# A retention block and a tanh-shrink MLP on one core: weights first, and another order of the opening

## The chip, the cores and the metric

The kernel runs on one core of one Trainium2 chip. A core has TensorE (matrix products, PE in the profile; its weight loads are PEld), VectorE (DVE), ScalarE (ACT), GpSimd (POOL) and SyncE (SP), which here only issues DMA transfers. Each engine works through its own instructions in order; semaphores tie them together. The metric is device time in microseconds, the median over runs.

## The reference

Inputs are q, k, v of shape (4, 8, 768, 64) in float32, w_in of (512, 2048) and w_out of (2048, 512), both in float64, and the output is (3072, 512) in float32.

```python
gamma = 1.0 - 2.0 ** (-5.0 - np.arange(H))          # H = 8 heads
for t in range(S):                                   # S = 768, D = 64
    state = gamma * state + k[:, :, t] (outer) v[:, :, t]
    y[:, :, t] = (1 / sqrt(D)) * q[:, :, t] @ state
x = y.transpose(0, 2, 1, 3).reshape(B * S, H * D)    # 3072 x 512
h = x @ w_in                                         # 3072 x 2048
out = (h - tanh(h)) @ w_out                          # 3072 x 512
```

## The kernel before

**Chunks.** The 3072 tokens are 24 chunks of 128; six chunks make one batch entry. A chunk's k, q and v are 128 tokens x 512 (8 heads of 64). The decay is folded into q and v: they are multiplied by tables of powers of gamma (`scale`, L236). k and q are turned so that a head's 64 features lie on partitions, either by TensorE (`turn`, L250, four 128x128 transposes each for k and q, then copied to SBUF by ScalarE in `turn_copy`, L262 and L264) or by a DMA that transposes 16-bit words (`turn_by_dma`: ScalarE splits the words into the buffer `apart`, L273; SP writes them to DRAM, L276, and reads them back transposed, L278). `apart` has one buffer. Then `products` makes k'v for the state and k q' for the scores (L298, L304, 32 passes each), VectorE masks the scores (L311) and adds up the state (L321 to L327), and `outputs` with `outputs_rest` forms y in PSUM (L352). `see` reads four single columns of it on ScalarE (L382), which orders the second part behind the first, and `keep_x` copies y to xT (L393), four chunks to a tile.

**Weights.** There are 32 weight tiles of 512 KB as float64. Tiles come in eights: four of w_in (128 columns each), then four of w_out (128 rows each). A tile is loaded by SP, in three DMAs for w_in and one for w_out (L154, L149). It is turned into float32 by hand: ScalarE takes the two words apart (`convert_begin`, L172, L173), VectorE puts the bits together in four instructions (`convert_bits`, L181 to L187), and GpSimd or VectorE does the last multiply and add (`convert_end`, L195, L199). The first three tiles, and those from 9 on, use three staging buffers; tiles 3 to 8 use spare room that later holds xT.

**Steps.** The MLP goes in 96 steps, each 256 tokens (n) by 256 hidden columns (m2). `up` is two half steps of eight passes (L414) into one PSUM bank of tag `h`, of which there are two. ScalarE makes the square, the tanh and three factors (`shrink_begin`, `shrink_factors`, L423 to L433); VectorE does six instructions (`shrink_multiply`, `shrink_end`, L439 to L453), the fifth of which is the last to read the bank. `down` is eight passes of 128x512 (L462), two steps later in the plain loop. The first steps go (0,0), (0,1), (1,0), (1,1), (2,0), (2,1), (3,0), (3,1); step 8 is (3,2).

**The order.** Steps 0 to 7 and chunks 0 to 7 are written out by hand as a string of pieces, a letter and a number each, which are emitted in that order to all engines' queues. L loads a chunk, W a weight tile, s and w scale q and v, t and T turn k and q, c and C copy what was turned, K turns by DMA, p, m and z are products, mask and state, b, e, r and y are the outputs, `see`, the rest and the copy to xT. A, D and G are the three parts of a conversion. u and v are a step's two half steps, a, q, d and g its four parts on ScalarE and VectorE, o its down and E the copy of its sums. x counts zero products that the next group of PE work runs ahead of itself: `keep_busy` multiplies a tile of zeros, in a PSUM bank that is about to be overwritten. From step 8 on (`BEGUN`) a plain loop sets the order, and chunks from 8 on are turned by DMA.

PSUM banks of tag `t` (the later turned k and q, and the products) are one pair, so each group waits until the last has been read. k and q have two SBUF buffers each, v four, so SP's load of chunk 2 waits until chunk 0 has been used, and what is behind it on SP waits too. SP also waits, before each DMA, for the eighth DMA before it.

Of the kernel before, what the change touches and what calls it, by code (L numbers as in the profile page):

```python
# [16 lines left out]
P = 128  # L17
# [7 lines left out]
B0, C0 = 1.1162213056058772, 5.494931718829769  # L25
B1, C1 = -1.609711559785289, 5.546157850574988
# [6 lines left out]
def kernel(  # L33
# [20 lines left out]
    nc = tc.nc  # L54
# [28 lines left out]
    def bank(tag, name):  # L83
        return ps.tile([P, BANK], F32, tag=tag, name=name)
# [8 lines left out]
    at = [0]  # L93
# [6 lines left out]
    busy = cst.tile([P, P], F32, name="busy")  # L100
# [9 lines left out]
    w1 = wts.tile([P, NC, DF], F32, name="w1")  # L110
    w2 = wts.tile([P, NM, DM], F32, name="w2")
# [78 lines left out]
    def convert_end(i, engine):  # L190
        if i not in words:
            return
        dst, src = weight_ends(i)
        head, low, power = words.pop(i)
        engine.tensor_tensor(low, low, power.bitcast(F32), op=ALU.mult)  # L195
        head = head.bitcast(F32)
        if isinstance(src, list):
            low, head = (t.rearrange("p (c n) -> p c n", c=NC) for t in (low, head))
        engine.tensor_tensor(dst, low, head, op=ALU.add)  # L199
# [5 lines left out]

    idle = [0]

    def keep_busy(at):  # L210
        for _ in range(idle[0]):
            nc.tensor.matmul(at, busy, busy, start=True, stop=True, skip_group_check=True)  # L212
        idle[0] = 0


    loaded = {}
# [15 lines left out]
    def scale(ci, which, engine):  # L232
        if ci >= NCH:
            return
        t, g = loaded[ci][1 + which], (gq, gv)[which]
        engine.tensor_tensor(t, t, g[:, ts(ci % CPB, H)][:, :, None].to_broadcast([P, H, D]),  # L236
                             op=ALU.mult)

    def turn(ci, which, early=False):

        if early:
            tp = bank("o", f"kqTp{which}_{ci}")
        else:
            if which == 0:
                turned[ci] = banks("t", f"kqTp_{ci}")
            tp = turned[ci][:, which]
        keep_busy(tp[:, :P])
        t = loaded[ci][which]
        for p in range(NP):
            nc.tensor.transpose(tp[:, ts(p, P)],  # L250
                                t[:, ds(2 * p, 2)].rearrange("p h d -> p (h d)"), ident)
        if early:
            turned.setdefault(ci, []).append(tp)
# [31 lines left out]
    scores = {}  # L285

    def products(ci):

        kh, _, vh = loaded[ci]
        kT, qT = (sides[ci][:, i] for i in range(2))  # L290
        sp = banks("t", f"s_{ci}")
        keep_busy(sp[:, 0, :P])
        scores[ci] = halves = sp.rearrange("p r (w n t) -> p r w n t", w=2, n=NP)
        for p in range(NP):
            for a in range(2):
                for i in range(2):
                    h, r = 2 * p + i, ds(D * a, D)
                    nc.tensor.matmul(halves[ds(D * i, D), a, 1, p], kh[r, h], vh[r, h],  # L298
                                     start=True, stop=True, skip_group_check=True)
        for p in range(NP):  # L300
            for a in range(2):
                for i in range(2):
                    r = ds(D * i, D)
                    nc.tensor.matmul(halves[ds(D * a, D), i, 0, p], kT[r, p, ts(a, D)],  # L304
                                     qT[r, p, ts(a, D)], start=True, stop=True,
                                     skip_group_check=True)
# [7 lines left out]
        masked[ci] = m  # L314

    def state(ci):
        halves = scores.pop(ci)
        j = ci % CPB
        if j == 0:
            states[ci] = mid.tile([P, 2, NP, D], F32, tag="state", name=f"state_{ci}", bufs=3)  # L320
            nc.vector.tensor_copy(states[ci][:, 1], halves[:, 0, 1])  # L321
        else:
            nc.vector.tensor_tensor(states[ci][:, 1], halves[:, 0, 1], states[ci][:, 0],
                                    op=ALU.add)
        if j < CPB - 1:
            nxt = mid.tile([P, 2, NP, D], F32, tag="state", name=f"state_{ci + 1}", bufs=3)
            nc.vector.tensor_tensor(nxt[:, 0], halves[:, 1, 1], states[ci][:, 1], op=ALU.add)  # L327
            states[ci + 1] = nxt
# [7 lines left out]
    def outputs(ci):  # L336

        j = ci % CPB
        vh = loaded[ci][2]
        turned.pop(ci, None)  # L340
        qT = sides.pop(ci)[:, 1]
        a_, st = masked.pop(ci), states.pop(ci)
        y = y_banks[:, ci % 2]
        keep_busy(y[:, 0, 0])
        begun = set()

        def to_y(p, i, a, lhsT, rhs):

            col, r = (i + p) % 2, (ci + p) % 2
            start = (r, col) not in begun  # L350
            begun.add((r, col))
            nc.tensor.matmul(y[ds(D * col, D), r, p // 2, ts(a, D)], lhsT, rhs,  # L352
                             start=start, stop=True, skip_group_check=True)

        def intra(first):
            for pp in range(NP // 2):
                for i in range(2):
                    for a in range(2):

                        for col in range(2):  # L360
                            p = 2 * pp + ((a + col) % 2 if first else (a + col + 1) % 2)
                            if (i + p) % 2 != col:
                                continue
                            r = ds(D * a, D)
                            to_y(p, i, a, vh[r, 2 * p + i], a_[r, i, p])

        for a in range(2):
            if j or a:
                for p in range(NP):
                    for i in range(2):  # L370
                        r = ds(D * i, D)
                        to_y(p, i, a, st[r, a, p], qT[r, p, ts(a, D)])
        intra(True)
        halfway[ci] = intra
# [25 lines left out]
    o_p = {}  # L400
# [6 lines left out]
    def up(n, m2, i):  # L407

        if i == 0:
            hps[n, m2] = bank("h", f"h_{n}_{m2}")  # L410
        hp = hps[n, m2][:, ts(i, TH)]
        keep_busy(hp[:, :P])
        for c in range(NC):
            nc.tensor.matmul(hp, w1[:, c, ts(2 * m2 + i, P)], xT[n // 2][:, c, ts(n % 2, TH)],  # L414
                             start=(i == 0 and c == 0), stop=(c == NC - 1),
                             skip_group_check=True)
# [39 lines left out]
    def down(n, m2, j, first, last):  # L456

        if first:
            o_p[j] = bank("o", f"o_{n}_{m2}_{j}")
            keep_busy(o_p[j][:, :P])  # L460
        for i in range(2):
            nc.tensor.matmul(o_p[j], gT[n, m2][:, i, ts(j, P)], w2[:, 2 * m2 + i],  # L462
                             start=(first and i == 0), stop=(last and i == 1))
# [74 lines left out]

    BEGUN = 8
    EARLY_TURNS = 4  # L540
    TO_VECTOR = 2

    def tall(ci):
        return nc.vector if ci < TO_VECTOR else nc.gpsimd

    pieces = {
        "L": load_chunk,
        "W": load_weights,
        "s": lambda c: scale(c, 0, tall(c)),
        "w": lambda c: scale(c, 1, tall(c)),  # L550
        "t": lambda c: turn(c, 0, c < EARLY_TURNS),
        "T": lambda c: turn(c, 1, c < EARLY_TURNS),
        "c": lambda c: turn_copy(c, 0),
        "C": lambda c: turn_copy(c, 1 if c < EARLY_TURNS else None),
        "K": turn_by_dma,
        "p": products,
        "m": mask,
        "z": state,
# [3 lines left out]
        "y": keep_x,  # L562
        "A": convert_begin,
        "D": convert_bits,
        "G": lambda i: convert_end(i, tall(i)),
        "u": lambda s: up(*steps[s][:2], 0),
        "v": lambda s: up(*steps[s][:2], 1),
        "a": lambda s: shrink_begin(*steps[s][:2]),
# [3 lines left out]
        "o": lambda s: [down(*steps[s][:2], j, *steps[s][2:]) for j in range(2)],  # L572
        "E": lambda s: [add_up(*steps[s][:2], j) for j in range(2)],
        "x": lambda n: idle.__setitem__(0, n),
    }
    if w_out.dtype != F32:
        rooms += [xp.tile([P, 2, 2 * BANK], U32, tag="xT", name=f"raws_{i}") for i in range(3)]
    order = """
    L0 x8 t0 c0 s0 x5 T0 w0 L1 C0 x3 t1 W0 p0 c1 s1 m0 x2 T1 z0 W1 C1 w1 x3 b0 p1 e0 A0 r0
    m1 z1 y0 A1 D0 L2 x4 b1 t2 e1 c2 G0 r1 s2 y1 D1 x3 T2 w2 L3 u0 C2 W2 p2 G1 s3 t3 m2 T3  # L580
    w3 c3 v0 z2 C3 b2 A2 L4 p3 e2 W3 D2 a0 r2 s4 y2 w4 q0 W4 m3 z3 G2 x9 t4 b3 A3 d0 T4 e3
    C4 r3 g0 L5 y3 x1 p4 A4 W5 u2 D3 s5 v2 W6 w5 m4 D4 u1 G3 a2 q2 z4 L6 x6 t5 d2 G4 T5 A5
    v1 W7 C5 g2 b4 s6 a1 W8 p5 w6 e4 u3 D5 q1 L7 W9 W10 W11 K6 v3 m5 A6 G5 z5 r4 a3 d1 b5 y4 e5
    o0 s7 g1 w7 A7 D6 q3 K7 r5 D7 G6 y5 x3 u4 d3 v4 G7 A8 g3 p6 a4 o1 A9 m6
    z6 q4 D8 p7 E1 d4 G8 b6 o2 e6 m7 g4 A10 r6 z7 u5 y6 D9 b7 v5 D10 G9 e7 r7 a5 o3 y7 q5
    G10 u6 E3 d5 A11 v6 g5 o4 a6 D11 q6 u7 G11 d6 v7 g6 o5 a7 q7 E5 d7 g7 W12 L8 W13 W14
    """
    for piece in order.split():
        pieces[piece[0]](int(piece[1:]))
# [10 lines left out]
    for s in range(BEGUN, len(steps)):  # L600
        n, m2, first, last = steps[s]
        ci = with_chunk.get(s)
# [86 lines left out]
```

## Time and profile before

| | |
|---|---|
| median of 3 runs | 759.88 us (759.51 to 760.18) |
| profiled execution, its own time | 760.18 us |
| its span | 758.2 us |
| TensorE busy | 741.9 us, 98% |
| VectorE busy | 518.5 us, 68% |
| ScalarE busy | 391.3 us, 52% |
| GpSimd busy | 126.2 us, 17% |
| zeros on TensorE (L212) | 94 passes: 72, 14, 6 and 2 by the bank they are written to |
| DMA | 61.86 MB, mean 82 GB/s |

The busy shares are means over two parts with different limits: the opening, which ends where step 8 starts, and the plain loop after it. Zero products count as busy time. A matmul of float32 shows as two passes, so eight passes of a 128x256 product are four matmuls. In the order of time, the duration of a group of matmuls includes the end of the last one, and groups overlap by about 0.15 us; the cost of a group is taken from start to start.

### The profile page before, as it was taken

How to read it: one execution, taken by the hardware profiler on the slowest of the kernel's cores; microseconds unless marked ns; L12 is line 12 of the kernel's file. 1: busy time of each engine (PE TensorE's matmuls, PEld its weight loads, DVE VectorE, ACT ScalarE, POOL GpSimd, SP SyncE). 2: the span in 40 equal slices, each digit the busy share in tenths (PEclk: the TensorE clock that was granted, in tenths of full speed). 3: DMA queues.
4: the chain of work that ended last, by engine and by line, in shares of the span. 5: the costliest groups of instructions: out<-in, count | busy, mean ns of one | idle time of the engine just before them, and what ended most of it. 6: DMA issues, size and time to landing. Idle time of an engine off the chain costs nothing.

```text
span 758.2 us, 13865 instructions
## 1 busy us (share of the span) xinstructions
PE 741.9 (98%) x5486; PEld 510.0 (67%) x5486; DVE 518.5 (68%) x807; ACT 391.3 (52%) x729; POOL 126.2 (17%) x108
## 2 busy tenths in 40 slices
PE   8896999999999999999999999999999999999998
PEld 7774666767676767666767666766666666666775
DVE  4896979998898667565656565655655665656653
ACT  3675577676666464445464455343444344434442
POOL 0573425544534111001111000000000000000000
PEclk9998999999999999999999999999999999999999
DMA  9976417655642434323432422000000000000000
GB/s 192 230 203 166 99 56 182 181 145 154 162 141 69 126 108 118 96 74 80 127 76 64 126 56 57 29 1 1 28 1 0 29 0 1 29 0 1 28 2 28
DMA packets 130129, 61.86 MB, mean 82 GB/s; under 512 B 114065, under 2 KB 122769, under 8 KB 130065
## 3 DMA queue, kind: packets, MB, share of 16 engines
q1 hardware_dynamic: 129776, 60.77, 30.9%
q8 instruction: 43, 0.70, 0.4%
q10 hardware_dynamic: 288, 0.21, 0.1%
q14 instruction: 22, 0.17, 0.1%
HBM read 35.80 MB, written 15.73 MB: 68 GB/s over the span
## 4 chain that ended last, share of the span: by engine, by line
PE 95%; DVE 3%; ACT 1%; issue 0%; DMA 0%; POOL 0%; DVEq 0%; POOLq 0%
PE h L414 43%; PE o L462 41%; PE y L352 3%; PE o L470 2%; PE s L298 2%; PE s L304 1%; PE kqTp L212 1%; PE kqTp L250 1%; DVE head L185 1%; DVE head L183 1%; DVE power L187 0%; DVE head L181 0%; PE y L212 0%; DVE a L311 0%; DMA out_dram<-sum 0%
## 5 line engine op out<-in xcount | busy, mean ns | idle before, releaser
L414 PE MATMUL h<-xT,w 128*128 128x256 f32 x1536 | 352.3, 382 | 6.6 <-ACT xT L393 6.6
L414 PEld LDWEIGHTS h<-xT,w 128*128 128x128 f32 x1536 | 291.4, 191 | 75.9 <-issue 31.8
L462 PE MATMUL o<-w,g 128*128 128x512 f32 x736 | 332.0, 593 | 0.0
L462 PEld LDWEIGHTS o<-w,g 128*128 128x128 f32 x736 | 139.4, 190 | 135.1 <-issue 128.9
L423 ACT ACTIVATE u<-h 128x512 f32<-128x512 f32 x96 | 57.3, 597 | 291.3 <-PE h L414 291.2
L439 DVE TENSOR_TENSOR th<-h,th 128x512 f32<-128x512 f32 x96 | 66.3, 690 | 176.9 <-ACT th L424 176.9
L453 DVE COPY_PREDICATED g<-large,th 128x512 f32<-128x512 int32 x96 | 72.0, 750 | 9.9
L442 DVE SCALAR_TENSOR_TENSOR h<-q,h 128x512 f32<-128x512 f32 x96 | 66.9, 696 | 10.0
L448 DVE SCALAR_TENSOR_TENSOR h<-q,h 128x512 f32<-128x512 f32 x96 | 66.6, 694 | 8.6 <-DVE h L442 0.5
L431 ACT ACTIVATE q<-u,tab 128x512 f32<-128x512 f32 x96 | 69.4, 723 | 0.0
L432 ACT ACTIVATE q<-u,tab 128x512 f32<-128x512 f32 x96 | 69.1, 720 | 0.0
L433 ACT ACTIVATE large<-u,tab 128x512 f32<-128x512 f32 x96 | 68.8, 716 | 0.0
L452 DVE TENSOR_TENSOR g<-h,u 128x512 f32<-128x512 f32 x96 | 66.3, 691 | 3.3
L440 DVE SCALAR_TENSOR_TENSOR h<-u,h 128x512 f32<-128x512 f32 x96 | 65.8, 685 | 0.0
L236 POOL TENSOR_TENSOR q<-q,tab 128x512 f32<-128x512 f32 x22 | 23.7, 1077 | 199.4 <-DMA q<-in_q_dram 173.7
L424 ACT ACTIVATE th<-h 128x512 f32<-128x512 f32 x96 | 56.8, 592 | 0.0
L195 POOL TENSOR_TENSOR low<-low,power 128x512 f32<-128x512 f32 x30 | 38.6, 1287 | 108.4 <-DVE power L187 89.2
L199 POOL TENSOR_TENSOR w<-low,head 128x512 f32<-128x512 f32 x30 | 38.7, 1290 | 2.4
L352 PEld LDWEIGHTS y<-a,v 64*64 64x64 f32 x768 | 16.1, 136 | 16.2 <-ACT large L433 10.6
L236 POOL TENSOR_TENSOR v<-v,tab 128x512 f32<-128x512 f32 x22 | 26.2, 1190 | 0.6 <-DMA v<-in_v_dram 0.4
L382 ACT COPY seen<-y 64x1 f32<-64x1 f32 x96 | 10.1, 154 | 27.4 <-PE y L352 27.0
L393 ACT COPY xT<-y 128x512 f32<-128x512 f32 x24 | 14.1, 587 | 17.1 <-PE y L352 17.1
(54 smaller groups left out, 411.7 us busy)
## 6 DMA issues: line engine op xcount, KB each, us to landing
rows<-apart SPq DMA_DIRECT2D x18, 512.0 KB, 2.7
k<-in_k_dram SPq DMA_DIRECT2D x24, 256.0 KB, 4.3
q<-in_q_dram SPq DMA_DIRECT2D x24, 256.0 KB, 4.9
v<-in_v_dram SPq DMA_DIRECT2D x24, 256.0 KB, 5.2
raw<-in_moe_w_out_dram SPq DMA_DIRECT2D x12, 512.0 KB, 3.5
out_dram<-sum SPq DMA_DIRECT2D x23, 256.0 KB, 2.1
raw<-in_moe_w_in_dram SPq DMA_DIRECT2D x14, 256.0 KB, 4.1
raw<-in_moe_w_in_dram SPq DMA_DIRECT2D x28, 128.0 KB, 4.1
```

Source lines behind the costliest of these rows:

```text
L414: nc.tensor.matmul(hp, w1[:, c, ts(2 * m2 + i, P)], xT[n // 2][:, c, ts(n % 2, TH)], start=(i == 0 and c == 0), stop=(c == NC - 1), skip_g ...
L423: nc.scalar.activation(u, hp, AF.Square)
L431: nc.scalar.activation(q0, u, AF.Square, bias=bias0)
L432: nc.scalar.activation(q1, u, AF.Square, bias=bias1, scale=math.sqrt(A))
L433: nc.scalar.activation(large, u, AF.Relu, bias=bias_m)
L439: nc.vector.tensor_tensor(th, hp, th, op=ALU.subtract)
L440: nc.vector.scalar_tensor_tensor(hp, in0=u, scalar=R, in1=hp, op0=ALU.subtract, op1=ALU.mult, reverse0=True)
L442: nc.vector.scalar_tensor_tensor(hp, in0=q0, scalar=C0, in1=hp, op0=ALU.add, op1=ALU.mult)
L448: nc.vector.scalar_tensor_tensor(hp, in0=q1, scalar=A * C1, in1=hp, op0=ALU.add, op1=ALU.mult)
L452: nc.vector.tensor_tensor(flat, hp, u, op=ALU.mult)
L453: nc.vector.copy_predicated(flat, large.bitcast(I32), th)
L462: nc.tensor.matmul(o_p[j], gT[n, m2][:, i, ts(j, P)], w2[:, 2 * m2 + i], start=(first and i == 0), stop=(last and i == 1))
```

## The change

- K6 and K7 are gone: chunks 6 and 7 are turned by TensorE and copied by ScalarE, as chunks 4 and 5 were.
- SP loads the weight tiles 0, 1 and 2 ahead of chunk 0, and their conversions begin ahead of it. A piece X runs zeros at once in a bank of tag `h`; 40 units stand before the first transpose, and 7, 3, 1 and 2 later.
- A zero product may be up to 512 columns wide, with the 128 columns of zeros broadcast. A "unit" is 128 columns.
- VectorE scales chunks 0 and 4, where it was 0 and 1; GpSimd the others. Conversions 0 and 1 still end on VectorE.
- The order of all pieces of the first eight steps is another. Step 8 and everything behind it is as before.

```diff
     def keep_busy(at):
-        for _ in range(idle[0]):
-            nc.tensor.matmul(at, busy, busy, start=True, stop=True, skip_group_check=True)
-        idle[0] = 0
+        most = at.shape[-1] // P
+        while idle[0]:
+            n = min(idle[0], most)
+            zeros = busy[:, None, :].to_broadcast([P, n, P])
+            nc.tensor.matmul(at[:, : n * P].rearrange("p (n t) -> p n t", n=n), busy, zeros,
+                             start=True, stop=True, skip_group_check=True)
+            idle[0] -= n
...
-        keep_busy(tp[:, :P])
+        keep_busy(tp)
...
-        halves = scores.pop(ci)
+        halves = scores[ci]
...
-        keep_busy(y[:, 0, 0])
...
-    TO_VECTOR = 2
-
-    def tall(ci):
-        return nc.vector if ci < TO_VECTOR else nc.gpsimd
+
+    SCALED = {0, 4}
+    ENDED = {0, 1}
+
+    def engine(i, among):
+        return nc.vector if i in among else nc.gpsimd
...
-        "s": lambda c: scale(c, 0, tall(c)),
-        "w": lambda c: scale(c, 1, tall(c)),
+        "s": lambda c: scale(c, 0, engine(c, SCALED)),
+        "w": lambda c: scale(c, 1, engine(c, SCALED)),
...
-        "K": turn_by_dma,
...
-        "G": lambda i: convert_end(i, tall(i)),
+        "G": lambda i: convert_end(i, engine(i, ENDED)),
...
+        "X": lambda n: (idle.__setitem__(0, n), keep_busy(bank("h", "zeros"))),
...
-    L0 x8 t0 c0 s0 x5 T0 w0 L1 C0 x3 t1 W0 p0 c1 s1 m0 x2 T1 z0 W1 C1 w1 x3 b0 p1 e0 A0 r0
-    m1 z1 y0 A1 D0 L2 x4 b1 t2 e1 c2 G0 r1 s2 y1 D1 x3 T2 w2 L3 u0 C2 W2 p2 G1 s3 t3 m2 T3
-    w3 c3 v0 z2 C3 b2 A2 L4 p3 e2 W3 D2 a0 r2 s4 y2 w4 q0 W4 m3 z3 G2 x9 t4 b3 A3 d0 T4 e3
-    C4 r3 g0 L5 y3 x1 p4 A4 W5 u2 D3 s5 v2 W6 w5 m4 D4 u1 G3 a2 q2 z4 L6 x6 t5 d2 G4 T5 A5
-    v1 W7 C5 g2 b4 s6 a1 W8 p5 w6 e4 u3 D5 q1 L7 W9 W10 W11 K6 v3 m5 A6 G5 z5 r4 a3 d1 b5 y4 e5
-    o0 s7 g1 w7 A7 D6 q3 K7 r5 D7 G6 y5 x3 u4 d3 v4 G7 A8 g3 p6 a4 o1 A9 m6
-    z6 q4 D8 p7 E1 d4 G8 b6 o2 e6 m7 g4 A10 r6 z7 u5 y6 D9 b7 v5 D10 G9 e7 r7 a5 o3 y7 q5
-    G10 u6 E3 d5 A11 v6 g5 o4 a6 D11 q6 u7 G11 d6 v7 g6 o5 a7 q7 E5 d7 g7 W12 L8 W13 W14
+    W0 W1 W2 A0 D0 L0 A1 G0 D1 A2 L1 D2 X40 t0 W3 c0 s0 w0 X7 T0 t1 G1 C0 p0 c1 s1 z0 L2 m0
+    w1 X3 T1 b0 G2 e0 C1 p1 z1 A3 r0 L3 m1 t2 y0 D3 W4 c2 b1 s2 e1 X1 r1 T2 w2 y1 C2 X2 p2
+    s3 t3 m2 c3 z2 w3 L4 T3 b2 W5 C3 G3 p3 e2 A4 r2 m3 u0 z3 y2 L5 s4 t4 D4 b3 T4 v0 C4 w4
+    e3 r3 p4 y3 z4 s5 a0 u2 m4 q0 G4 L6 d0 W6 t5 W7 b4 A5 T5 w5 g0 v2 W8 C5 e4 u1 a2 D5 W9
+    q2 p5 z5 G5 r4 v1 y4 m5 d2 b5 a1 s6 t6 o0 e5 L7 g2 w6 A6 W10 q1 D6 T6 W11 u3 C6 d1 s7 p6
+    w7 r5 v3 z6 y5 G6 A7 m6 g1 t7 b6 T7 u4 C7 D7 e6 a3 p7 z7 G7 A8 r6 v4 m7 y6 q3 d3 b7 o1
+    a4 g3 A9 q4 d4 u5 e7 g4 r7 v5 y7 E1 u6 D8 a5 q5 o2 d5 G8 g5 A10 v6 D9 u7 a6 q6 o3 D10 d6
+    G10 v7 E3 g6 G9 o4 a7 q7 d7 A11 o5 g7 D11 E5 G11 W12 L8 W13 W14
```

More of the change, by code (lines that the diff above doesn't have):

```diff
@@ L291, in products @@
         sp = banks("t", f"s_{ci}")
-        keep_busy(sp[:, 0, :P])
+        keep_busy(sp[:, 0])
         scores[ci] = halves = sp.rearrange("p r (w n t) -> p r w n t", w=2, n=NP)
@@ L411, in up @@
         hp = hps[n, m2][:, ts(i, TH)]
-        keep_busy(hp[:, :P])
+        keep_busy(hp)
         for c in range(NC):
@@ L459, in down @@
             o_p[j] = bank("o", f"o_{n}_{m2}_{j}")
-            keep_busy(o_p[j][:, :P])
+            keep_busy(o_p[j])
         for i in range(2):
```

## The prediction

> **What bounds the kernel now.** I read the chain that ended last, then the busy time in two windows, then what TensorE waited for, and then the order of time on the engines around each wait.
>
> ```profile
> PE 95%; DVE 3%; ACT 1%; issue 0%; DMA 0%; POOL 0%; DVEq 0%; POOLq 0%
> ```
> ```profile
> 0.00:105.00 105.00, 92.33 (x1311) 70.31 (x1312) 80.31 (x125) 59.16 (x124) 40.32 (x36) 0.95 0.71 166
> 105.00:758.20 653.20, 649.57 (x4177) 439.69 (x4175) 438.21 (x682) 332.12 (x606) 85.91 (x72) 1.00 0.25 68
> ```
> The columns of the second fence are the window, its length, busy time (and instructions) of TensorE, its weight loads, VectorE, ScalarE and GpSimd, TensorE's granted clock, the DMA share and GB/s. Step 8, the first of the plain loop, starts at 104.99. From there TensorE is busy 649.6 of 653.2 us at full clock, and the change touches nothing of it. So the opening's 105 us decide, and there the 92.33 of TensorE hold zeros and slow matmuls:
>
> ```profile
> 1.05 3.79 PE L212 MATMUL kqTp<-busy 128*128 128x128 f32 x16 [1.05 <-DVE busy L101]
> 4.78 1.09 PE L250 MATMUL kqTp<-tab,k 128*128 128x128 f32 x4
> 15.98 1.59 PE L212 MATMUL y<-busy 128*128 128x128 f32 x8 [0.68 <-ACT xT L393]
> 17.50 1.13 PE L352 MATMUL y<-kqT,state 64*64 64x64 f32 x32
> 27.29 0.69 PE L352 MATMUL y<-kqT,state 64*64 64x64 f32 x32
> 66.20 6.15 PE L414 MATMUL h<-xT,w 128*128 128x256 f32 x16 [6.64 <-ACT xT L393]
> 104.99 3.62 PE L414 MATMUL h<-xT,w 128*128 128x256 f32 x16
> ```
> The 6.64 us wait is the largest; after it one step's products take 6.15 where others take 3.45 (start to start), because the clock had dropped. What held ScalarE's copy of x back:
>
> ```profile
> 52.53 6.24 SPq L154 DMA_DIRECT2D raw<-in_moe_w_in_dram  x9
> 58.87 0.54 SPq L276 DMA_DIRECT2D rows<-apart  x1
> 63.49 1.87 SPq L278 DMA_TRANSPOSE kqT<-rows  x1
> ```
> ```profile
> 63.55 1.05 ACT L273 COPY apart<-k 128x1024 uint16<-128x1024 uint16 x1 [3.92 <-DMA rows<-apart]
> 64.50 1.04 ACT L273 COPY apart<-q 128x1024 uint16<-128x1024 uint16 x1
> 65.57 0.58 ACT L393 COPY xT<-y 128x512 f32<-128x512 f32 x1
> ```
> Chunk 7's split (K7) needs the one `apart` buffer, which chunk 6's write holds, and that write was queued behind nine weight loads on SP. ScalarE is in order, so y5 stands behind K7, and u4 behind y5.
>
> ```profile
> 17.14 0.69 DVE L195 TENSOR_TENSOR low<-low,power 128x512 f32<-128x512 f32 x1
> 22.21 1.34 DVE L195 TENSOR_TENSOR low<-low,power 128x512 f32<-128x512 f32 x1
> 23.59 1.42 DVE L199 TENSOR_TENSOR w<-low,head 128x512 f32<-128x512 f32 x1
> ```
> VectorE's SBUF work takes twice as long beside GpSimd. Thirteen such instructions before 105 us (in conversions 1, 4, 6, 7 and 10) lose 10.9 us together against their short forms.
>
> ```profile
> GB/s 57 249 218 257 252 172 141 243 201 147 276 256 235 254 270 242 312 33 131 188 260 238 238 81 299 52 146 0 6 0 3 244 243 186 60 131 0 0 0 13
> ```
> These are slices of 2.75 us of the first 110: the DMA engines move about 250 GB/s when the queue lets them.
>
> **The change part by part.** I work out when step 8 starts.
>
> Zeros. A wide zero matmul does four units of 128 columns; 128x512 products run 3.43 us for 8 passes, two passes each, so 0.86 per four units, 0.21 each. Narrow ones took 0.67 for three, 0.22 each. The width is free; only the number counts (47 units before, 53 after, 40 of them at the start).
>
> Opening. Nine SP issues (W0, W1, W2: 1.57 MB) now stand ahead of the first chunk, so k0 waits for them. Tables and first chunk, 0.94 MB, had landed at 7.08; two pieces more by 9.49, 218 GB/s. At 230 (218 here, 250 in the slices) I get W0 5.9, W1 8.2, W2 10.5, k0 11.6, q0 12.8, v0 13.9, k1 15.1, q1 16.2, v1 17.3, W3 19.6. The 40 units begin at 1.05; slow until 5.87 as before (0.47 each, ten units), then thirty at 0.215: 12.3. So the first transpose starts at 12.3 instead of 4.84: a loss of 7.5. Bounds: 11.6 (k0 alone) and 15.2 (k0 at the 166 GB/s of the window).
> The Trainium skill, "TensorE: Matmul & The Clock Gate", section "What's actually happening", has the slow clock last some 3.4 us of work; by that the zeros would end at 11.5 and k0 at 11.6 would decide, 0.7 less. The row's 4.8 us is used.
>
> From the first transpose to u0. These pieces are chunks 0 to 2 whole, and chunk 3 up to its products. TensorE's own work: 8 transposes of 0.44, 4 x 1.09 (products), 3 outputs (0.47, 0.70, 0.70), 3 rests of 0.39, 13 zero units: 13.8. Upper bound: the same took 4.84 to 29.38 before, less u0 and v0 (2 x 1.73): 21.1. By hand between them, with VectorE in order (D0, G0, D1, D2 at 2.07, 1.42): D2 ends 14.6, s0 15.3, so T0 at 15.3; p0 ends 17.3. Chunk 1's scaling moves to GpSimd (1.1 and 1.2 instead of 0.69 each), 16.2 to 18.5, and beside it G1 on VectorE loses 0.65 + 0.73 as in the rows above: G1 ends 18.6, mask 0 at 20.0, b0 at 20.4, p1 (behind `see` 0.45 and its copy 0.58) 21.9, t2 22.8, b1 23.7, T2 25.0 (q2 lands 22, GpSimd scales it to 23.1). p2 26.5. L3's k waits on SP until p1 has read k1 (21.0), lands 4.3 later at 25.3, q3 26.4; its scaling and T3 28.0, v3's scaling 28.7, p3 and r2 30.0. So u0 at 30.0, 17.7 after the first transpose. D3 and m2 lie beside this, about 1 late with GpSimd's s2, w2.
> The Trainium skill, "SBUF — State Buffer", section "Who interferes with whom", speaks against putting this scaling on GpSimd: whichever engine starts first keeps the shared ports for its whole instruction. By that G1's two instructions could each lose a whole GpSimd multiply, 1.1 + 1.2, so 0.9 more than the rows say; the sum goes by the rows.
>
> From u0 to step 8. TensorE: 16 half steps of 1.73 (27.7), 6 downs of 3.43 (20.6), 8 transposes (3.5, of which chunks 6 and 7 are 1.8 of new work), 4 products (4.4), outputs of chunks 3 to 7 (3.2), 5 rests (2.0): 61.4. Changes of kind cost a little (half steps of 1.92 and downs of 3.63 after small matmuls): 1.3. Waits: VectorE's 70 us of work from 7.2 to g6 is a close second; u4 needs the bank of step 1, freed by g1, behind D6, which meets the scaling of chunk 7 on GpSimd; o1 needs weight 7 (W7), finished on GpSimd behind D7. I take 2.0. Bounds: 0, and 8 (the 10.9 of rows above less the 3 charged already).
>
> What goes: 4 splits of 1.04 on ScalarE (2 copies of 1.01 come, nearer their use), 4 SP issues, 2.1 MB, and with them the 6.64 wait and the 2.7 of slow clock. y5 then waits only for r5. Next late is the bank of step 1 above. Weight 14 waits for D11, which ends near step 8's start instead of ten us before, but its conversion is in step 9, 7 us on; free. Chunk 4's scaling, now on VectorE, costs it 1.4 and chunk 1's gives 1.4 back. G10 ahead of G9 on GpSimd ends G9 at about 88, before step 8 needs it.
>
> Clock. An idle 1.23 and 0.68 near 15 us were followed by eight zeros in 1.59 (0.89 warm) and outputs that took 0.6 more. The changed opening has several idle gaps of 0.3 to 0.8. Bounds 0 and 2.5; I take 0.8, since the gaps are shorter.
>
> Sum: 12.3 + 17.7 + 61.4 + 1.3 + 2.0 + 0.8 = 95.5, against 104.99: 9.5 less. Afterwards: VectorE reaches D12 2.25 after step 8's start now; step 10 (118.77) finds its bank freed at 116.73, 2.0 of slack. D11 and G11 now end about there, so D12 can be 2 to 3 late: 0 to 1, taken 0.3. Net 9.2. The profiled execution is the 760.18 run (span 758.2); 0.30 above the median of 759.88. So 751.0 for its like, 750.7 for the median.
>
> **The rivals.**
> VectorE bounds the opening. For: 80.31 busy of 105, and rows twice as long beside GpSimd. Against: it idles 6.1 us in the K7 stall and more later. Chain as before (+3.4) and waits of 6 instead of 2 (+4): 758.1 at the worst, 756 in the middle.
> DMA is slower than the slices (slower than before). Weights first, and chunk buffers that free late: at 166 GB/s k0 is 3.6 later, and v3 (5.4 MB) lands at 35.8 instead of 27.4. For: slices of 172 and 141. Against: those fall where SP waited for buffers; 235 to 312 follow. It decides below some 160 GB/s, where the 9 us are gone; at 145 v3 lands at 40.5, and the kernel takes 764.
> The chain runs at TensorE's pace: 12.3 + 13.8 + 62.7 + 1 = 89.8, so 745.
> The stall does not go: y5's place is taken by another ScalarE wait of equal size. Against: the pieces ahead of u4 need only transposes and copies; 759.5.
>
> **How the numbers follow.** What a measurement can tell from no change is 0.2%, 1.5 us. Forecast (746.5 to 754) 0.60; TensorE's pace 0.11; VectorE 0.16; DMA, slower, 0.10; no change 0.03. Faster: 0.60 + 0.11 + 0.16 = 0.87. The range leaves out the best half of the pace case and DMA with the worst: 745.5 to 757.5.
>
> **What would show it.** First transpose near 12.3; u0 near 30; no wait above 1.5 us between 30 and 95, ScalarE's L393 gone from TensorE's waits; step 8 near 95.5; about 653 from there to the end. I am wrong if k0 lands after 14, if TensorE waits for VectorE by more than 5 us in all after u0, or if the stretch after step 8 grows by over 1.5.

## The result, and the profile after

The changed kernel takes 754.41 us (median of 6 runs, 753.45 to 755.44), the kernel before 760.22 us (759.51 to 761.23) beside it. The ratio is 0.9923, with a 95% interval of 0.9910 to 0.9936: 5.8 us faster, where 9.2 were forecast for the median (9.5 at the start of step 8). The profiled execution took 755.44 us, 1.0 above its median, with a span of 753.7 us. So the mechanism was there and a part of the gain was missing.

The chain of work that ended last, by engine, in the profile after:

```profile
PE 92%; DVE 5%; issue 1%; DMA 1%; ACT 1%; POOL 0%; SPq 0%; DVEq 0%; ACTq 0%; POOLq 0%
```

VectorE has grown from 3% to 5% of the chain. Busy time in four windows, cut at the first transpose, at step 0's first half (u0), and at step 8 (columns: window, length, TensorE, its weight loads, VectorE, ScalarE and GpSimd with their instructions, granted clock, DMA share, GB/s):

```profile
0.00:11.97 11.97, 10.92 (x20) 4.69 (x21) 3.95 (x9) 4.09 (x6) 0.20 (x4) 1.00 0.91 202
11.97:33.57 21.60, 17.13 (x475) 13.43 (x473) 14.46 (x25) 9.97 (x28) 12.30 (x10) 0.92 0.89 195
33.57:99.62 66.05, 64.28 (x772) 45.55 (x769) 54.51 (x95) 43.18 (x89) 24.14 (x20) 1.00 0.52 123
99.62:753.70 654.08, 649.85 (x4177) 439.62 (x4175) 438.75 (x681) 332.18 (x605) 88.03 (x74) 1.00 0.26 69
```

Step 8 starts at 99.62 instead of 104.99, and the loop after it takes 654.1 instead of 653.2. The lengths can be held against the sum directly: 11.97 (forecast 12.3), 21.60 (17.7), 66.05 (65.5), and 0.9 more in the loop (0.3). One line is off, the second, and it is the only one whose granted clock is below 1. (In the first, the trace has no clock record before 5.59, and the zeros ahead of that time run at half speed.) What TensorE waited for in the whole opening, the longest first (total, times, longest):

```profile
PE kqTp L256 <- DVE q L242: 2.1, 1, 2.1
PE y L357 <- issue: 1.2, 1, 1.2
...
PE s L310 <- ACT kqT L270: 0.7, 1, 0.7
...
PE s L304 <- issue: 0.6, 1, 0.6
PE s L310 <- issue: 0.5, 1, 0.5
```

The copy of x that held TensorE for 6.64 us is gone from the list. At its head is now a wait for VectorE, in the missed window. TensorE's order of time there (start, duration, operation, count, and in brackets the idle time before it with its releaser):

```profile
11.97 0.60 PE L256 MATMUL kqTp<-tab,k 128*128 128x128 f32 x4
...
16.13 0.66 PE L256 MATMUL kqTp<-tab,q 128*128 128x128 f32 x4 [2.05 <-DVE q L242]
...
22.65 1.13 PE L310 MATMUL s<-kqT 64*64 64x64 f32 x32 [0.71 <-ACT kqT L270]
...
24.14 1.11 PE L256 MATMUL kqTp<-tab,k 128*128 128x128 f32 x4
25.18 1.07 PE L357 MATMUL y<-kqT,state 64*64 64x64 f32 x32
...
33.08 0.27 PE L310 MATMUL s<-kqT 64*64 64x64 f32 x2 [0.53 <-issue]
...
33.57 1.99 PE L419 MATMUL h<-xT,w 128*128 128x256 f32 x8
```

Two things are to be seen. T0, the turning of q of chunk 0, comes 0.8 later than worked out (16.13 against 15.3). And from 22.65 to 26.09 the pieces run at half speed: 1.13, 1.11 and 1.07 where the same forms take 0.65, 0.60 and 0.69 a little later. Why T0 is late is on ScalarE and VectorE:

```profile
5.91 1.28 ACT L172 ACT_TABLE_LOAD   x1 [5.91 <-DMA raw<-in_moe_w_in_dram]
7.20 0.67 ACT L172 ACTIVATE head<-raw 128x512 f32<-128x512 f32 x1
```
```profile
7.91 0.43 DVE L181 TENSOR_SCALAR head<-head 128x512 f32<-128x512 f32 x1 [6.91 <-ACT head L172]
...
13.41 0.42 DVE L181 TENSOR_SCALAR head<-head 128x512 f32<-128x512 f32 x1
...
15.39 0.68 DVE L242 TENSOR_TENSOR q<-q,tab 128x512 f32<-128x512 f32 x1
...
16.59 1.53 DVE L195 TENSOR_TENSOR low<-low,power 128x512 f32<-128x512 f32 x1
18.16 1.41 DVE L199 TENSOR_TENSOR w<-low,head 128x512 f32<-128x512 f32 x1
```

ScalarE's first instruction that needs its function table is now the conversion of weight tile 0, and the 1.28 us load of that table stands between the tile's landing (5.9) and that conversion. VectorE therefore starts D0 at 7.91, and its third conversion (D2, 13.41 to 15.4) stands ahead of the scaling of q. The wait, the table load and the order of D2 can each be changed alone.

### The profile page after: what moved, and what is told of

Its sections match the earlier page's. It is cut to its first block, busy times and chain, and to the rows that moved or that the text cites. A ratio compares the mean times of both kernels' runs of the same rounds, so it can differ in the third digit from the quotient of the medians.

```text
span 753.7 us, 13758 instructions
## 1 busy us (share of the span) xinstructions
PE 742.2 (98%) x5438; PEld 503.3 (67%) x5438; DVE 511.7 (68%) x807; ACT 389.4 (52%) x727; POOL 124.7 (17%) x108
## 4 chain that ended last, share of the span: by engine, by line
PE 92%; DVE 5%; issue 1%; DMA 1%; ACT 1%; POOL 0%; SPq 0%; DVEq 0%; ACTq 0%; POOLq 0%
PE h L419 43%; PE o L467 40%; PE y L357 4%; PE o L475 2%; PE s L310 2%; PE s L304 2%; PE kqTp L256 1%; DVE head L185 1%; DVE head L183 1%; DMA raw<-in_moe_w_in_dram 1%; DVE head L181 0%; DVE power L187 0%; DVE g L458 0%; DVE low L195 0%; DVE h L447 0%
## 5 line engine op out<-in xcount | busy, mean ns | idle before, releaser
L357 PEld LDWEIGHTS y<-a,v 64*64 64x64 f32 x768 | 16.2, 136 | 15.3 <-ACT large L438 10.6
L242 POOL TENSOR_TENSOR v<-v,tab 128x512 f32<-128x512 f32 x22 | 25.3, 1149 | 2.0 <-DMA v<-in_v_dram 2.0
```

## The experiments

Line numbers move by one where a kernel has a line more. Each time is a median, and each ratio is to the kernel before, run on the same chip. The runs were made on more than one chip, so ratios are compared across runs, and medians only as far as they go.

### Was it the DMA turn, or the new order? (e1, e2, e10, e9)

**e1: the order of before, with chunks 6 and 7 turned by TensorE.**

```diff
-    v1 W7 C5 g2 b4 s6 a1 W8 p5 w6 e4 u3 D5 q1 L7 W9 W10 W11 K6 v3 m5 A6 G5 z5 r4 a3 d1 b5 y4 e5
-    o0 s7 g1 w7 A7 D6 q3 K7 r5 D7 G6 y5 x3 u4 d3 v4 G7 A8 g3 p6 a4 o1 A9 m6
-    z6 q4 D8 p7 E1 ...
+    v1 W7 C5 g2 b4 s6 a1 W8 p5 w6 e4 u3 D5 q1 L7 W9 W10 W11 v3 m5 A6 G5 z5 r4 t6 T6 C6 a3 d1 b5 y4 e5
+    o0 s7 g1 w7 A7 D6 q3 r5 D7 G6 y5 x3 u4 d3 v4 G7 A8 g3 p6 a4 o1 A9 m6
+    z6 t7 T7 C7 q4 D8 p7 E1 ...
```

> The order of before, its loads and its zeros, with one part of the change alone: chunks 6 and 7 are turned by TensorE (t6 T6 C6 behind r4, t7 T7 C7 behind z6) and K6, K7 are gone. If the removed wait is the whole gain: u4 starts near 60.5 instead of 66.2 at full clock, 6 to 9 us less on that wait and the slow clock, 1.8 more for the transposes, so 5 to 7.5 us less than before, 753 to 755: as good as the changed kernel. If instead the new order of the opening carries the gain, and the wait of 6.64 only moves to VectorE (conversions 6 and 7, step 3), then 0 to 2 us less, 758 to 760.

Measured: 755.61 us, ratio 0.9951 (0.9938 to 0.9963), 4.0 us faster. TensorE's order of time around the old stall:

```profile
61.32 3.72 PE L414 MATMUL h<-xT,w 128*128 128x256 f32 x16 [0.86 <-ACT xT L393]
```

The 6.64 is down to 0.86, and step 4's products take 3.72 instead of 6.15: the half speed went with the wait. Step 8 starts at 100.49. So this edit alone gives 4.0 us, beside 5.8 for the whole change.

**e2: the new order, with chunks 6 and 7 turned by DMA.** K6 stands behind u3 and K7 behind u4.

```diff
-    q2 p5 z5 G5 r4 v1 y4 m5 d2 b5 a1 s6 t6 o0 e5 L7 g2 w6 A6 W10 q1 D6 T6 W11 u3 C6 d1 s7 p6
-    w7 r5 v3 z6 y5 G6 A7 m6 g1 t7 b6 T7 u4 C7 D7 ...
+    q2 p5 z5 G5 r4 v1 y4 m5 d2 b5 a1 s6 o0 e5 L7 g2 w6 A6 W10 q1 D6 W11 u3 K6 d1 s7 p6
+    w7 r5 v3 z6 y5 G6 A7 m6 g1 b6 u4 K7 D7 ...
```

> The changed kernel with K6 and K7 put back (K6 behind u3, K7 behind u4, where C6 and C7 stood; no t6, T6, t7, T7). If the removed wait is the gain: chunk 7's split waits for chunk 6's write again, some 4 to 5 us on ScalarE, u6 or a3 late, and the time is 3 to 8 us above the changed kernel's 754.4, so 757 to 762. If the new order alone carries the gain: 1.8 us less of transposes and no new wait, 752.5 to 754.

Measured: 769.62 us, ratio 1.0133 (1.0119 to 1.0148), 10 us slower than before, and beyond both forecasts. SyncE's queue and TensorE's order of time:

```profile
54.37 5.02 SPq L154 DMA_DIRECT2D raw<-in_moe_w_in_dram  x6
59.49 0.54 SPq L282 DMA_DIRECT2D rows<-apart  x1
```
```profile
67.86 1.13 PE L310 MATMUL s<-kqT 64*64 64x64 f32 x32 [8.79 <-DMA kqT<-rows]
...
80.02 1.13 PE L310 MATMUL s<-kqT 64*64 64x64 f32 x32 [4.64 <-DMA kqT<-rows]
```

In the new order the products follow so soon that TensorE waits for both round trips, 13.4 us together, and each wait is followed by matmuls at half speed (1.13 where 0.65 is the form). Again six weight loads stand ahead of the first write.

**e10: the same, with the DMA turns put earlier.** K6 stands behind the load of chunk 7, ahead of the weight loads 10 and 11, and K7 behind the scaling of q of chunk 7.

```diff
-    ... a1 s6 t6 o0 e5 L7 g2 w6 A6 W10 q1 D6 T6 W11 u3 C6 d1 s7 p6
-    w7 r5 v3 z6 y5 G6 A7 m6 g1 t7 b6 T7 u4 C7 D7 ...
+    ... a1 s6 o0 e5 L7 K6 g2 w6 A6 W10 q1 D6 W11 u3 d1 s7 K7 p6
+    w7 r5 v3 z6 y5 G6 A7 m6 g1 b6 u4 D7 ...
```

> The changed kernel with K6 and K7 put back as early as q is scaled: K6 behind L7 and ahead of weights 10 and 11, K7 behind s7. If the queue made the DMA turn expensive in the changed order: chunk 6 turned at 62 to 65 instead of 67.9, the waits of 8.8 and 4.6 fall to 2 to 4 in all, 755 to 758. If the way there and back (write, transpose, some 8 us from split to use) is too long wherever it is queued: waits of 8 or more in all stay, 763 to 768.

Measured: 763.55 us, ratio 1.0047 (1.0031 to 1.0063). The waits are about halved (7.4 us together, 13.4 in e2), not gone:

```profile
64.54 1.13 PE L310 MATMUL s<-kqT 64*64 64x64 f32 x32 [4.37 <-DMA kqT<-rows]
...
76.00 0.79 PE L310 MATMUL s<-kqT 64*64 64x64 f32 x32 [3.04 <-DMA kqT<-rows]
```

The split of chunk 6 began at 54.69 and its products at 64.54: some 10 us lie between them, although its write was issued at 56.71, as soon as the split had ended. Chunk 7's write stood behind six weight loads again (its split ended at 62.27, the write was issued at 66.06), so the second wait is at least in part a matter of the queue. TensorE's own turn of k and q costs it 0.9 us a chunk. The new order gains together with the turn on TensorE; with either place of the DMA turn that was tried it loses.

**e9: the kernel before, with the loads of three weight tiles moved behind the second DMA turn.** This leaves the DMA turn and changes its place in SyncE's queue; the nine loads come later by it.

```diff
-    ... D5 q1 L7 W9 W10 W11 K6 v3 m5 A6 G5 z5 r4 a3 d1 b5 y4 e5
-    o0 s7 g1 w7 A7 D6 q3 K7 r5 D7 ...
+    ... D5 q1 L7 K6 v3 m5 A6 G5 z5 r4 a3 d1 b5 y4 e5
+    o0 s7 g1 w7 A7 D6 q3 K7 W9 W10 W11 r5 D7 ...
```

> The kernel before, with its DMA transposes and its order, and one thing moved: the loads of weights 9, 10 and 11 (nine issues on SP) stand behind K7 instead of ahead of K6. If the wait of 6.64 comes from the place of chunk 6's write in SP's queue: that write issues near 53.4 instead of 58.87, chunk 7's split ends 5 us earlier, u4 waits 0 to 2 and the clock stays up: 753 to 755. If the write and the transposes are slow in themselves: u4 waits 5 or more as before, 758 to 760.

Measured: 756.78 us, ratio 0.9966 (0.9954 to 0.9977), 2.6 us faster. SyncE issues the write at 53.47 (58.87 before). TensorE:

```profile
62.17 3.72 PE L414 MATMUL h<-xT,w 128*128 128x256 f32 x16 [2.61 <-ACT xT L393]
...
75.24 3.70 PE L462 MATMUL o<-w,g 128*128 128x512 f32 x8 [3.07 <-ACT sum L499]
```

The stall falls from 6.64 to 2.61 and the half speed behind it is gone: of the 9.3 us that both cost, 4.0 + 2.4 were a matter of the nine weight loads that stood ahead of one write. But a new wait of 3.07 for ScalarE's copy of the sums stands at the down after it, and gives about half of that back. It comes from the moved loads: SyncE issues them from 66.39 on, and ScalarE, which works in order, waits for one of them ahead of the copy:

```profile
71.65 0.68 ACT L172 ACTIVATE head<-raw 128x512 f32<-128x512 f32 x1 [4.64 <-DMA raw<-in_moe_w_in_dram]
```

In e1, where these loads stay early, the wait for the sums is 0.7. So the queue place is shown as the cause of most of the stall. In these two orders of the queue either the write or the weights come late, and taking the turn off the queue avoids both.

The new order by itself, weights first included, is then the difference between e1 and the changed kernel: 0.9951 against 0.9923, some 2 us, with intervals that only just do not overlap (0.9938 and 0.9936 are their near ends). That it gains by itself is therefore indicated and not firmly shown.

### What the first transposes wait for (e3, e4, e7)

**e3: the table load early.** A copy of two columns on ScalarE, right after the zeros are written, makes ScalarE load its table while nothing has landed yet.

```diff
     nc.vector.memset(busy, 0.0)
+    nc.scalar.copy(out=seen, in_=busy[:, :2])
```

> The changed kernel with one two-column copy on ScalarE ahead of everything, so that the table load of 1.28 us runs at the start instead of behind the first weight tile's landing. If the opening is tied to ScalarE's and VectorE's first conversions: D0 at 6.6 instead of 7.9, T0 0.8 to 1.3 earlier, u0 and step 8 as much earlier: 753.1 to 753.6. If the chunk loads or TensorE's clock set the opening: 754.4, no change.

Measured: 753.74 us, ratio 0.9918 (0.9903 to 0.9933). ScalarE's first instructions:

```profile
1.19 1.28 ACT L102 ACT_TABLE_LOAD   x1 [1.19 <-PEq L679]
...
6.36 0.66 ACT L173 ACTIVATE head<-raw 128x512 f32<-128x512 f32 x1 [3.68 <-DMA raw<-in_moe_w_in_dram]
```

The load is out of the way, conversion 0 starts 0.84 earlier (the tile itself landed 0.5 later in this execution), T0 starts at 15.28, which is what I had worked out, and u0 at 31.93. In four profiles of this opening with the load where the changed kernel has it, T0 is at 16.13 (above), 16.30 (e2), 16.54 (e5) and 16.83 (e10).

**e4: conversion 2 later.** D2 moves behind chunk 0's mask, and G2 behind chunk 3's copies.

```diff
-    W0 W1 W2 A0 D0 L0 A1 G0 D1 A2 L1 D2 X40 t0 ... z0 L2 m0
-    w1 X3 T1 b0 G2 e0 ... C3 G3 p3 e2
+    W0 W1 W2 A0 D0 L0 A1 G0 D1 A2 L1 X40 t0 ... z0 L2 m0 D2
+    w1 X3 T1 b0 e0 ... C3 G2 G3 p3 e2
```

> The changed kernel with D2 behind m0 on VectorE instead of ahead of s0, and G2 ahead of G3 on GpSimd instead of behind chunk 1's scaling, so that the third weight tile no longer stands ahead of chunk 0. If VectorE's order sets the opening: T0 2.0 earlier, at 14.1, no wait of 2 us before it, and with it no drop of the clock near 22 to 26; u0 2 to 4 us earlier: 750.5 to 752.5. If chunk loads set it: T2 and later wait for q2 and q3 as before, 0 to 1 less: 753.4 to 754.4.

Measured: 753.28 us, ratio 0.9914 (0.9899 to 0.9929). TensorE's order of time:

```profile
14.54 0.66 PE L256 MATMUL kqTp<-tab,q 128*128 128x128 f32 x4 [0.21 <-DVE q L242]
...
21.72 0.66 PE L256 MATMUL kqTp<-tab,k 128*128 128x128 f32 x4 [0.30 <-DMA k<-in_k_dram]
...
27.84 0.66 PE L256 MATMUL kqTp<-tab,q 128*128 128x128 f32 x4 [0.81 <-POOL q L242]
...
30.45 1.99 PE L419 MATMUL h<-xT,w 128*128 128x256 f32 x8
```

The 2.05 us wait is 0.21, u0 is at 30.45 and step 8 at 96.41 (99.62). The clock stays at 1.00 from 6.1 on; it does so in e3 too, where 0.97 of the wait is left.

**e7: both.** The two edits above in one kernel.

> The changed kernel with both the early table load and D2, G2 late. If VectorE's order in front of chunk 0 was all: the two gains add, D0 at 6.6, T0 at 13.5 to 14.3, 752.0 to 752.7. If chunk loads set the pace once D2 is out of the way (t1 waited 0.34 for k1, t2 0.30 for k2, T2 0.81 for q2 with D2 late): no more than D2 late alone, 753 to 753.5.

Measured: 753.00 us, ratio 0.9903 (0.9890 to 0.9916). It is the lowest median of all, 7.4 us under the kernel before on the same chip, though its interval still overlaps that of the changed kernel. TensorE's waits in the opening:

```profile
PE y L358 <- issue: 1.1, 1, 1.1
...
PE s L305 <- issue: 0.9, 1, 0.9
PE kqTp L257 <- POOL q L243: 0.9, 1, 0.9
...
PE kqTp L257 <- DMA k<-in_k_dram: 0.6, 2, 0.3
```

No wait for VectorE is left behind the zeros; u0 starts at 30.83 and step 8 at 97.17. In time, none of the three edits is shown to gain on the changed kernel: the ratios are 0.9918, 0.9914 and 0.9903 against 0.9923, all with overlapping intervals, and e5 below, which leaves the wait where it is, has 0.9909. Nor does an earlier step 8 in one profile settle it: e5's is at 97.79 in the order of the changed kernel, where that one's was at 99.62. What the three show is which wait each edit takes away. The profile also tells what comes next: once VectorE is early, the chunks' own landing is next (`DMA k`), and then GpSimd's scaling of a chunk that landed late.

### Loads in the order of need (e8, e11)

**e8: weight tile 2 behind chunk 2, tile 3 behind chunk 3, fewer zeros.** With the early table.

```diff
-    W0 W1 W2 A0 D0 L0 A1 G0 D1 A2 L1 D2 X40 t0 W3 c0 s0 w0 X7 T0 ...
-    w1 X3 T1 b0 G2 e0 C1 p1 z1 A3 r0 L3 m1 t2 y0 D3 W4 ...
+    W0 W1 A0 D0 L0 A1 G0 D1 L1 X28 t0 c0 s0 w0 X3 T0 ...
+    w1 X1 T1 b0 e0 C1 p1 z1 W2 r0 L3 m1 t2 y0 W3 ...
```

> The changed kernel with the early table load and the third and fourth weight tiles loaded (and converted) behind chunks 1 and 2, where only step 1 at 42 us needs them; 28 units of zeros at the start instead of 40, 3 instead of 7 behind the first transpose. If the chunk loads are what is left of the opening: k0 lands near 9.5 and k1 near 13, the first transpose at 9.7, u0 at 28 to 29 instead of 33.6, 749 to 751. If VectorE's total work sets it, the conversions only come later: u0 earlier, but steps 1 and 3 wait, 752.5 to 754.5.

Measured: 754.89 us, ratio 0.9933 (0.9921 to 0.9945), no better than the changed kernel. The first transpose was at 9.52 and T0 at 12.71, 2.4 and 3.4 us earlier. But tile 2 now stood ahead of chunk 3 on SyncE, k of chunk 3 landed only at 25.4, no earlier than in the changed kernel (25.5), and u0 was at 31.67; step 8 at 98.70. The half speed is in this profile too, from 28.84 to 32.25.

**e11: tiles 2 and 3 behind chunk 3, their conversions behind the first products of step 0, steps 0 and 2 ahead of chunk 4.**

```diff
-    w1 X3 T1 b0 G2 e0 C1 p1 z1 A3 r0 L3 m1 ... u0 z3 y2 L5 s4 t4 D4 b3 T4 v0 C4 w4
-    e3 r3 p4 y3 z4 s5 a0 u2 m4 q0 G4 L6 d0 ...
+    w1 X1 T1 b0 e0 C1 p1 z1 L3 W2 r0 m1 ... u0 z3 y2 b3 D2 v0 e3 A3 r3 y3 a0 G2 L5 u2 D3 q0
+    s4 t4 A4 T4 v2 C4 w4 d0 G3 p4 D4 a2 z4 s5 m4 G4 L6 g0 ...
```

> The early table load, weights 2 and 3 loaded behind chunk 3, their conversions behind z3, and steps 0 and 2 (which need weights 0 and 1 only) both ahead of chunk 4. If chunk loads set the pace up to u0: k3 lands near 22 instead of 25.5, u0 at 28 to 29, step 8 at 94 to 96: 749.5 to 752. If VectorE has no room left for the conversions moved back, step 1 waits for weights 2 to 5 and the gain is lost: 753 to 756.

Measured: 755.47 us, ratio 0.9949 (0.9934 to 0.9963), some 2 us slower than the changed kernel by the ratios, with intervals that just overlap. TensorE's order of time:

```profile
29.03 1.99 PE L420 MATMUL h<-xT,w 128*128 128x256 f32 x8
...
44.02 0.63 PE L257 MATMUL kqTp<-tab,k 128*128 128x128 f32 x4 [3.11 <-issue]
```

u0 came at 29.03, 4.5 us before that of the changed kernel, and step 8 at 99.93, 0.3 after it. All of the gain went into pauses and waits in between, the largest 3.11 us. An early u0 is therefore not worth its time by itself: what counts is that the work behind it is ready too. The profile names no releaser for the 3.11 us, but the program and VectorE's order of time do. The piece is the turn of chunk 5, and it uses the pair of banks that the products of chunk 4 leave when VectorE has masked them. That mask ends at 43.92. On VectorE it stands behind conversion 4 (40.38 to 42.54), which was moved there, and on TensorE the turn now follows the products with no step between them:

```profile
43.24 0.68 DVE L318 TENSOR_TENSOR a<-s,tab 128x512 f32<-128x512 f32 x1
```

In e8 the same turn starts 0.10 us after the same mask too (43.38 and 43.48), behind a wait of 1.74. This fits the second of the two forecasts, that VectorE has no room for the conversions that were moved back, though it was not tried with the conversion taken away again.

### The zeros (e5, e6)

**e5: zero matmuls of 128 columns, as many units as in the changed kernel.**

```diff
-        most = at.shape[-1] // P
+        most = 1
```

> The changed kernel with every zero product 128 columns wide again (53 instead of 15 matmuls, the same columns). If the width is free, as the rows say (0.86 for four units against 0.22 for one): first transpose at 12.0 and 754.4, within 1. If the number of TensorE instructions matters for its unexplained pauses (0.53, 0.56 and 1.21 in the changed kernel): the pauses sit at other instructions and the time moves by 1 to 2 either way.

Measured: 753.37 us, ratio 0.9909 (0.9895 to 0.9923). The 40 units take 10.95 us as 80 narrow passes against 11.08 as 20 wide ones. The width costs or brings nothing that can be measured. This profile is of use for another reason: it has the order of the changed kernel, a wait for VectorE that is longer than there, and full clock from 4.8 on.

```profile
16.54 0.66 PE L256 MATMUL kqTp<-tab,q 128*128 128x128 f32 x4 [2.43 <-DVE q L242]
```

**e6: no zeros at all.** The computation is the same; zeros are never read.

```diff
     def keep_busy(at):
+        idle[0] = 0
```

> The changed kernel without any zero product. If VectorE and the chunk loads alone set the opening: T0 again near 16, u0 near 33.6, 754.4 within 0.7. If the clock matters there: the transposes and products from 12 on run at half clock until some 4 us of dense work have passed, p0 to b1 take 2 to 4 us longer, 756.5 to 758.5.

Measured: 755.45 us, ratio 0.9934 (0.9922 to 0.9946), 0.8 us more than with them by the ratios, within what the intervals allow to be nothing. TensorE's first two pieces:

```profile
12.26 1.08 PE L257 MATMUL kqTp<-tab,k 128*128 128x128 f32 x4 [12.26 <-DMA k<-in_k_dram]
16.89 1.11 PE L257 MATMUL kqTp<-tab,q 128*128 128x128 f32 x4 [3.55 <-DVE q L243]
```

They run at half speed (1.08 for 0.60), and the pieces up to 20.5 too, which costs about 2 us of TensorE's time, 0.5 of it ahead of a wait that is there anyway. Against it stands that this execution has no half speed later. It also shows that k of chunk 0 landed at 12.2 here; in the changed kernel it landed at 11.53, so zeros and transfer end within half a microsecond of each other.

## Why the prediction was right, and where it was off

**What goes: right.** The 6.64 us wait and the 2.7 us of half speed are gone, y5's copy holds nobody, and e1 and e9 show that they hung on the DMA turn, and that its place behind the weight loads was most of it. "The stall does not go" is refuted: there is no wait over 1.3 us between 34 us and the end of the profiled execution.

**Opening: right.** 12.3 was forecast for the first transpose and 11.97 measured, by the row of before and not the bound of 15.2: the transfers came at 200 GB/s and above (k of chunk 0 landed at 11.53 where 11.6 was worked out, k of chunk 3 at 25.50 where 25.3 was). That refutes the rival of a slower DMA. The zeros were slow until 5.59, where I took 5.87 from the rows of before; the clock record of before has 6.30.

**From the first transpose to u0: the term that was mis-sized.** 17.7 was taken, 13.8 to 21.1 were its bounds, and 21.6 came, above the upper one. The steps that I gave by hand lose it as they go:

| | by hand | measured | late by |
|---|---|---|---|
| T0 | 15.3 | 16.13 | 0.8 |
| G1 ends | 18.6 | 19.57 | 1.0 |
| mask 0 ends | 20.0 | 20.96 | 1.0 |
| p1 ends | 21.9 | 23.56 | 1.7 |
| t2 ends | 22.8 | 25.18 | 2.4 |
| T3 ends | 28.0 | 30.65 | 2.6 |
| u0 | 30.0 | 33.57 | 3.6 |

The first 0.8 is the table load: before, it stood at a harmless place on ScalarE, and the diff that put a weight tile first put it on the path. I had not asked where it would go. e3 takes it away, and T0 is at 15.28. The half speed from p1 to b1 is 1.4: from 22.65 to 26.09 the pieces take 3.44 from start to start, and in e3, without its one wait, 2.03. (From T0 to u0, pauses left out, it is 16.9 here and 15.7 in e5, the same order at full clock: 1.2.) I had set 0.8 for the clock, in another term. The 0.53 pause just ahead of u0 was in no term. The rest, 0.9, is left by subtraction (1.0 in e5). It lies in the chain of mask, state, `see` and copies between the pieces, whose waits are 0.37, 0.59, 0.71 and 0.21 in the profile after and which I priced at its instructions alone. No profile of this order comes to 30.0: in e3, with T0 as forecast and full clock, u0 is still 1.9 late, behind waits of 0.64 for k of chunk 2 and 0.82 for GpSimd's scaling of q of chunk 3. e4 and e7, where D2 is out of the way, come to 30.45 and 30.83. That VectorE is late here is my rival "VectorE bounds the opening" in a small form: not the 756 of its middle, since behind u0 it did not hold TensorE at all.

**From u0 to step 8: right in the total, in part by luck.** 61.4 + 1.3 + 2.0 + 0.8 = 65.5 against 66.05. The 2.0 for waits were 1.8 long, but not where I put them: neither the bank of step 1 nor weight 7 made a wait. Two pauses without a releaser did (1.2 and 0.6). TensorE's own work took 64.3 where 62.7 was summed, and the 0.8 for the clock was not used, since the slow clock fell ahead of u0: two errors that nearly cancel.

**The loop: more than was taken, inside its bounds.** 0.9 against 0.3, bounds 0 and 1. One part is seen. I had called weight 14's conversion free, and nothing waits for it; but weight 15's, next behind it on GpSimd, ends at 125.10 and makes the down of step 9 wait 0.40 us.

```profile
125.16 2.84 PE L467 MATMUL o<-w,g 128*128 128x512 f32 x6 [0.40 <-POOL w L199]
```

For the remaining 0.5 I have no line of the profile.

**Zeros' width: right**, by e5. **GpSimd's scaling beside G1: right.** G1's two instructions took 1.53 and 1.41 for 0.69 each, a loss of 1.6 where the rows said 1.4. By the Trainium skill, "SBUF — State Buffer", section "Who interferes with whom", the estimate had been up to 2.3. The other weighing, by the Trainium skill, "TensorE: Matmul & The Clock Gate", section "What's actually happening", was decided by neither side: the clock records of the traces put the end of the slow clock 3.3 to 5.7 us after the first zero at 1.05, not the same in each execution (at 5.6 in the profile after, 4.7 in that of e3, 6.1 in that of e4, 4.35 in that of e11, 6.7 in that of e7, all from the start of the span), against the page's 3.4 us and the 4.8 of the row.

The sum closes: 4.1 late at step 8 and 0.6 in the loop, less 0.2 around the span, are the 4.4 by which the profiled execution missed its 751.0. It lay 1.0 above its own median, so the median missed by 3.7. How much of this the table load and D2 cost in time the runs do not fix: e7, without both, has its u0 0.8 and its step 8 1.7 later than forecast, but a ratio whose interval overlaps that of the changed kernel. The half speed, the pauses, the loop's growth and the chain's rest are read from the profiles alone.

The measured 754.41 lies inside the stated range, but 0.4 above the band of 746.5 to 754 that was called the forecast: the width kept for the rivals took it in. Of the signs named ahead, u0 near 30 and step 8 near 95.5 did not come; the first transpose, the absent waits behind u0 and the length of the loop did.

## What to carry to other kernels

When a stall stands behind a transfer, look at what is queued ahead of that transfer before judging the transfer itself, and then at what the same engine would be late with next: e9 moved the loads of three tiles and got 2.6 us, because ScalarE then waited for the moved loads; e1 took the turn off the queue and got 4.0. When a change gives an engine another first instruction, ask what that first instruction drags along (here a 1.28 us table load), and make it happen while everything waits for the first transfer anyway. In a chain through an in-order engine, what nobody waits for belongs behind what the next matmul waits for: moving one conversion (e4) took a wait of 2.05 us down to 0.21, though the gain in time is not clear of noise, and e11, with a conversion ahead of a mask that a matmul waits for, has a wait of 3.11 there. An early start of one step, by itself, is worth nothing (e8, e11).

## What the runs showed of the hardware that was not expected

**TensorE pauses at fixed counts of matmuls.** The waits that the profile gives to "issue" do not belong to a piece of work. Counted in TensorE's matmul records, they come at the same numbers whatever stands there: 475, 602 and 857 in the profile after; 475 and 602 with narrow zeros; 347 and 602 without zeros; 602 and 857 in e4. These are some 127 or 255 apart. (The kernel before, e1 and e9 have one such pause, at 222.) In e5 the narrow zeros, which leave later pieces where they were but shift which piece is number 475, moved the pause from the scores to the outputs of a chunk:

```profile
31.40 0.40 PE L357 MATMUL y<-a,v 64*64 64x64 f32 x12 [0.69 <-issue]
...
36.74 0.39 PE L357 MATMUL y<-kqT,state 64*64 64x64 f32 x11 [0.85 <-issue]
```

They last from 0.16 (e3) to 1.8 us (e2). The 3.11 of e11 and the 1.74 of e8 are not of them: they come at 652 and 644, behind a mask. What makes these pauses, and why some are long, no run here shows.

**The clock drops for 3.4 us or twice that, and not in each execution.** In the profile after, TensorE's granted clock is 0.50 for 3.4 us from 22.65 on, in this view by windows (window, length, TensorE busy, clock, DMA share, GB/s):

```profile
14.00:16.00 2.00, 0.08 (x1) 1.00 1.28 221
...
22.00:24.00 2.00, 1.35 (x48) 0.66 0.81 182
24.00:26.00 2.00, 2.00 (x42) 0.50 1.18 249
26.00:28.00 2.00, 1.79 (x50) 0.98 1.02 295
```

It begins over 6 us after the idle slice at 14 to 16 has ended. The other drops in these traces last 3.4 us (one each in before, e8, e10 and e11) or 6.8 (one each in before and e10, two in e2). The timed executions of this kernel have a mean granted clock of 0.997 (755.44 and 754.98 us) or 0.999 to 1.0 (753.45 to 754.44): two of six were some 1 us longer. That the wait for VectorE brings the drop would fit e3 and e4, where the wait is shorter and the profiled executions show none. But e5 and e10 wait longer at the same place (2.43 and 2.44 us against 2.05) and show no drop in the opening, and one execution of e7, without the wait, had 0.995 and was no slower. So the wait alone does not bring it. The drop goes with about 1 us of the profiled execution, and explains less of the median; what sets it off is not settled.
